# Second attention product as whole float32, two heads side by side on halves of TensorE's columns

## The chip, the cores and the metric

The kernel runs on one core of a Trainium2 chip. The metric is the device time of one execution in microseconds (us). Before the change the median of three runs is 637.88 us (636.99 to 638.83).

## The reference

Attention over pooled keys, then a channel mix (a gated feed-forward with a token shift). B = 8 batches, H = 8 heads, S = 576 tokens, D = 64; keys and values are averaged over groups of 8 tokens, so each head has 72 keys.

```python
k_p = k.reshape(B, H, Sp, pool, D).mean(axis=3)        # Sp = 576 / 8 = 72
v_p = v.reshape(B, H, Sp, pool, D).mean(axis=3)
scores = scale * np.matmul(q, k_p.transpose(0, 1, 3, 2))
attn = softmax(scores)                                  # over the 72 keys
x = np.matmul(attn, v_p)                                # then heads side by side: (B, S, 512)
xk = mu_k * x + (1.0 - mu_k) * x_prev                   # x_prev: x shifted by one token
xr = mu_r * x + (1.0 - mu_r) * x_prev
k = np.maximum(xk @ w_k, 0.0)                           # 512 -> 1024
out = sigmoid(xr @ w_r) * (k * k @ w_v)                 # 1024 -> 512
```

## The kernel before

The 4608 tokens are cut into 12 chunks of 384 (`CHUNKS`, L32). A chunk lies in one batch or, every third, crosses from one to the next (192 tokens each). A chunk has three tiles of 128 tokens; 36 tiles in all. Matrix products of the channel mix are made in a reduced float32 form (`F32R`), with each operand split into a high and a low part and three products for one; chunk 0 alone (`WHOLE`, L35) uses whole float32, since its weights arrive as words that must first be converted.

Per tile: `softmax` (L562) multiplies queries by pooled keys (L582, on TensorE, two heads at a time through a block-diagonal `kbd`), subtracts the maximum, takes exponentials, and multiplies by the reciprocal sums, the first 64 keys of each head into `pm` (L638) and the last eight into `px` (L632). `transposed` (L646) turns `pm` with four TensorE transposes (L657, two heads of 64 keys each fill 128 columns), and copies the result into a high part `pth` (ScalarE, L668) and a low part `ptl` (VectorE, L670). `transposed_rest` (L676) makes three copies of the last eight keys of four heads (`pr`, L688 and L690: high, low, high), turns them with two transposes of 96 columns (L696), and copies them into `ptr` (L703).

Per batch: `values` (L503) sums the pooled values and writes them into block-diagonal `vbd_h` and `vbd_l` (high and low); `last_values` (L536) does so for the last eight keys, in one masked tile `vbd_r` of 96 rows (L549), whose input is loaded three times over (`vr`, L396).

Per chunk and pair of heads g = 0 to 3: `attended` (L707) makes, on TensorE, three products of 128 x 128 (high-high, low-high, high-low) and one of 96 x 128 for the last keys (L739), accumulated in one bank; where a chunk crosses batches, each of the two stretches has its own four. In chunk 0 one whole-float32 product with `vbd_w` takes the place of the three. Then `shifted` (L746) makes the token shift: ScalarE L752, GpSimd L760 to L764, VectorE L771 (`xm`, or `xkh` and `xrh` in chunk 0), and `x_parts` (L783) splits the result. After that come `hidden` (L815: x by w_k), `gate` (L864: x by w_r, sigmoid), and `mixed` (L896: by w_v), whose result is multiplied by the gate (L905) and stored (L909).

Loads are issued on SyncE's queue in the order of the list `LOADS` (L39), then batch by batch; weights are converted by `convert` (L405: ScalarE, then four VectorE operations, L419 to L431) and split by `split` (L440).

The order of the work is set while the program is built. `Order` (L70) runs every step as a thread: a thread names what it needs (`need`), which buffer it takes (`take`), and on which engine the next instructions would run and how long they are reckoned to take. It picks the engine that could start first and, on it, the ready thread with the earliest due time (`tile_due`, `att_due`, `begin`, moved by `EARLIER`). The result is one fixed list of instructions for each engine; on the chip each engine goes through its own list in order and waits on semaphores.

Of the kernel before, what the change touches and what calls it, by code (L numbers as in the profile page):

```python
# [16 lines left out]
P = 128  # L17
# [3 lines left out]
KM = 64  # L21
# [6 lines left out]
REM = 3 * 4 * KR  # L28
# [28 lines left out]
COPIES_ON_ACT = 0  # L57

EARLIER = {
# [3 lines left out]
}  # L63
# [127 lines left out]
def attention_then_channel_mix(  # L191
# [10 lines left out]
    mask: bass.AP,  # L202
# [12 lines left out]
    def slots(kind, n, shape, dtype=F32, pool=None):  # L215
# [6 lines left out]
    mask_sb = const.tile([REM, 4], F32, name="mask_sb")  # L222
# [8 lines left out]
    vbd_h = [const.tile([P, NPAIR, P], F32R, name=f"vbd_h{i}") for i in range(2)]  # L231
    vbd_l = [const.tile([P, NPAIR, P], F32R, name=f"vbd_l{i}") for i in range(2)]
    vbd_w = sb.tile([P, NPAIR, P], F32, name="vbd_w", tag="xkl")
    vbd_r = [const.tile([REM, 2, 4, D], F32R, name=f"vbd_r{i}") for i in range(2)]

# [4 lines left out]
        "pth": [P, NPAIR, CH], "ptl": [P, NPAIR, CH], "ptr": [REM, 2, CH],  # L240
# [3 lines left out]
    def operand(kind, c):  # L244
        if (kind, c) not in operands:
            dtype = F32 if c in WHOLE and kind != "ptr" else F32R
            operands[kind, c] = sb.tile(shapes[kind], dtype, name=f"{kind}_{c}", tag=kind)
        return operands[kind, c]
# [4 lines left out]
    slots("rk", 2, [P, CH])  # L253
    slots("e", 2, [P, 2, 4, KEYS])
    slots("pm", 2, [P, 2, 4, KM])
    slots("px", 2, [P, 2, 4, KR])
    slots("pr", 2, [P, 2, 3, 4, KR], F32R)
    slots("mx", 2, [P, 2, 4, 1])
    slots("sm", 2, [P, 2, 4, 1])
    slots("vq", 1, [REM, 2, D], F32R)  # L260
    slots("tmp", 2, [P, WP])
# [4 lines left out]
    for tag, n in (("sl", 2), ("ptl", 1), ("xrl", 1)):  # L266
# [46 lines left out]
    def constants():  # L313
# [7 lines left out]
        yield "dve", 0.5, False  # L321
        nc.vector.memset(vbd_w, 0.0)
        order.make(("values clear", 0))
        for t in (vbd_h[1], vbd_l[1]):
            yield "pool", 0.5, False
            nc.gpsimd.memset(t.bitcast(F32), 0.0)
        order.make(("values clear", 1))

    def warm():

        zeros = yield take("tmp")
# [7 lines left out]
        order.give("tmp", zeros)  # L339
# [27 lines left out]
    def load(kind, i):  # L367
        if kind == "c":
            yield "sp", 1.0, False
            nc.sync.dma_start(out=mask_sb, in_=mask)  # L370
            nc.sync.dma_start(out=mu_sb, in_=mu)
            order.fetched("mask", 2)
# [32 lines left out]
    def convert(kind, i):  # L405
# [8 lines left out]
        ff = yield take("tmp")  # L414
# [20 lines left out]
        order.give("tmp", ff)  # L435
# [67 lines left out]
    def values(b, p):  # L503
        i = b % 2
        whole = b == 0 and 0 in WHOLE
        yield need(("v", 2 * b + p), ("attended", last_chunk[b - 2]) if b > 1 else ("values clear", b))
# [3 lines left out]
        gs = slice(2 * p, 2 * p + 2)  # L510
        yield "act", 0.41, False
        for h2 in range(2):
            r = slice(h2 * D, (h2 + 1) * D)
            nc.scalar.copy(out=(vbd_w if whole else vbd_h[i])[r, gs, r], in_=o[r])
        if not whole:
            yield "dve", 0.4, True
            for h2 in range(2):
                r = slice(h2 * D, (h2 + 1) * D)
# [5 lines left out]
        if whole:  # L524
            yield need(*[("attended", c) for c in WHOLE])
            yield act(2 * P)
            nc.scalar.copy(out=vbd_h[i][:, gs], in_=vbd_w[:, gs])
            yield dve(2 * P)
            nc.vector.tensor_tensor(
# [116 lines left out]
    def transposed(i):  # L646
# [3 lines left out]
        if c == 1:  # L650
            yield need(("early", "ptl", 0))
# [342 lines left out]
```

## Time and profile before

| | |
|---|---|
| median of 3 runs | 637.88 us (636.99 to 638.83) |
| profiled execution | 637.27 us, of which 635.5 us from the first to the last instruction (its span) |
| granted TensorE clock, mean | 0.997 |
| TensorE busy | 621.6 us (98%) |
| VectorE, ScalarE, GpSimd busy | 413.7, 334.2, 215.2 us (65%, 53%, 34%) |
| DMA engines | about full in the first 50 us, mostly idle after that |

The profile names engines PE (TensorE products), PEld (its weight loads), DVE (VectorE), ACT (ScalarE), POOL (GpSimd) and SP (SyncE; SPq is its queue of issues). Products overlap in TensorE's pipeline, so that the busy time of a group is more than its share of the span: what one costs is read from the distance between the starts of two neighbours. A line such as `128*64 128x144` gives the stationary operand's rows and columns, then the moving one's shape. `[1.11 <-DVE xkh L771]` at a row's end is idle time before it and what ended it.

### The profile page before, as it was taken

The numbers are of one execution on the slowest core, as the hardware profiler recorded it, in microseconds if no ns is written. First come the engines' busy times: TensorE is split into PE (matmuls) and PEld (weight loads), VectorE is DVE, ScalarE is ACT, GpSimd is POOL, SyncE is SP. The second block draws the span as 40 slices with busy tenths as digits, with TensorE's granted clock in tenths as the row PEclk, the third lists the DMA queues.
The fourth block names the chain that finished last, engine by engine and source line by source line (L and its number), as shares of the span: only waits on it lengthen the run. The fifth ranks groups of instructions, "written<-read, shape, count | busy, mean of one in ns | idle before, by whom it ended". The sixth has DMA issues, their size and how long they took to land.

```text
span 635.5 us, 9032 instructions
## 1 busy us (share of the span) xinstructions
PE 621.6 (98%) x3240; PEld 537.8 (85%) x3240; DVE 413.7 (65%) x829; ACT 334.2 (53%) x688; POOL 215.2 (34%) x331
## 2 busy tenths in 40 slices
PE   7899999999999999999999999999999999999997
PEld 6754468889989989989988988988988988988986
DVE  5999998856979537647845665855954654653421
ACT  4667656855665544635554555546555445444420
POOL 1240347464445128018115018316405104203200
PEclk9999999999999999999999999999999999999999
DMA  9991130043314211033011061033110100000001
GB/s 300 369 393 47 32 126 34 17 126 141 92 51 172 60 35 51 0 142 107 17 35 51 0 200 51 17 103 131 33 35 34 34 18 34 18 0 35 17 1 50
DMA packets 34988, 50.91 MB, mean 80 GB/s; under 512 B 6528, under 2 KB 22912, under 8 KB 34944
## 3 DMA queue, kind: packets, MB, share of 16 engines
q1 hardware_dynamic: 34944, 50.35, 23.6%
q8 instruction: 25, 0.41, 0.3%
q14 instruction: 19, 0.16, 0.1%
HBM read 40.90 MB, written 9.44 MB: 79 GB/s over the span
## 4 chain that ended last, share of the span: by engine, by line
PE 81%; DVE 8%; DMA 6%; POOL 2%; issue 1%; ACT 1%; SPq 1%; ACTq 0%; POOLq 0%; DVEq 0%
PE mm L896 28%; PE mm L815 26%; PE mm L864 15%; PE bank L739 5%; PE sc L582 4%; PE bank L657 2%; DMA qs<-in_qT 2%; DMA early_xrl<-in_vm 1%; DMA got_wk<-in_w_k 1%; DMA got_wv<-in_w_v 1%; PE bank L696 1%; DVE tmp L426 1%; DVE tmp L419 1%; DVE pr L688 1%; POOL xrl L789 1%
## 5 line engine op out<-in xcount | busy, mean ns | idle before, releaser
L815 PE MATMUL mm<-xkh,w_k 128*128 128x384 f32 x704 | 182.3, 339 | 0.3 <-ACT xkh L787 0.3
L896 PE MATMUL mm<-w_v,sh 128*128 128x512 f32 x528 | 170.8, 392 | 0.0
L815 PEld LDWEIGHTS mm<-xkh,w_k 128*128 128x128 f32 x704 | 125.6, 188 | 1.9 <-issue 0.6
L815 PE MATMUL mm<-xkl,w_k 128*128 128x384 f32 x352 | 118.2, 336 | 0.7 <-POOL xkl L789 0.7
L896 PEld LDWEIGHTS mm<-w_v,sh 128*128 128x128 f32 x528 | 99.2, 188 | 19.8 <-issue 0.2
L896 PE MATMUL mm<-w_v,sl 128*128 128x512 f32 x264 | 103.0, 390 | 0.0
L632 POOL TENSOR_TENSOR px<-e,sm 128x64 f32<-128x64 f32 x32 | 10.8, 339 | 225.0 <-DVE sm L626 224.8
L864 PE MATMUL mm<-w_r,xrh 128*128 128x512 f32 x264 | 84.9, 394 | 0.0
L752 ACT ACTIVATE t<-bank,om_sb 128x384 f32<-128x384 f32 x96 | 48.8, 582 | 55.9 <-PE bank L739 55.8
L838 ACT CAST sh<-rk 128x384 fp32r<-128x384 f32 x88 | 45.2, 514 | 58.7 <-DVE rk L832 58.7
L771 DVE SCALAR_TENSOR_TENSOR xm<-bank,mu_sb,t 128x384 f32<-128x384 f32 x88 | 51.4, 612 | 35.1 <-POOL t L764 18.3
L840 DVE TENSOR_TENSOR sl<-rk,sh 128x384 fp32r<-128x384 f32 x88 | 53.3, 609 | 25.5 <-ACT sh L838 25.4
L815 PEld LDWEIGHTS mm<-xkl,w_k 128*128 128x128 f32 x352 | 66.1, 188 | 1.3 <-POOL xkl L789 1.3
L905 DVE TENSOR_TENSOR rs<-mm,rs 128x512 f32<-128x512 f32 x36 | 24.8, 689 | 60.7 <-PE mm L896 60.7
L832 DVE SCALAR_TENSOR_TENSOR rk<-mm,rk 128x384 f32<-128x384 f32 x88 | 48.5, 552 | 16.3 <-ACT rk L825 15.9
L864 PEld LDWEIGHTS mm<-w_r,xrh 128*128 128x128 f32 x264 | 49.6, 188 | 10.0
L789 POOL TENSOR_TENSOR xkl<-xm,xkh 128x384 fp32r<-128x384 f32 x44 | 44.8, 1021 | 38.2 <-ACT xkh L787 37.9
L896 PEld LDWEIGHTS mm<-w_v,sl 128*128 128x128 f32 x264 | 49.7, 188 | 9.0
L463 POOL TENSOR_TENSOR stage<-stage 128x512 f32<-128x512 f32 (+5 forms) x60 | 50.7, 852 | 13.7 <-ACT rk L825 5.9
L825 ACT ACTIVATE rk<-mm 128x384 f32<-128x384 f32 x88 | 42.8, 487 | 23.4 <-PE mm L815 22.7
L864 PE MATMUL mm<-w_r,xrl 128*128 128x512 f32 x132 | 51.4, 389 | 0.0
L595 DVE TENSOR_REDUCE mx<-sc 128x8 f32<-128x576 f32 x35 | 26.3, 751 | 32.6 <-PE sc L582 32.6
(115 smaller groups left out, 977.7 us busy)
## 6 DMA issues: line engine op xcount, KB each, us to landing
out<-rs SPq DMA_DIRECT2D x36, 256.0 KB, 2.0
stage<-in_kT SPq DMA_DIRECT2D x15, 576.0 KB, 5.2
qs<-in_qT SPq DMA_DIRECT2D x32, 256.0 KB, 3.2
stage<-in_vm SPq DMA_DIRECT2D x14, 512.0 KB, 6.3
got_wk<-in_w_k SPq DMA_DIRECT2D x8, 512.0 KB, 8.6
got_wv<-in_w_v SPq DMA_DIRECT2D x8, 512.0 KB, 10.0
stage<-in_vr SPq DMA_DIRECT2D x7, 384.0 KB, 4.5
got_wr<-in_w_r SPq DMA_DIRECT2D x4, 512.0 KB, 8.4
```

What stands on the lines that cost most here:

```text
L463: nc_eng.tensor_tensor(out=st[:, :, :w], in0=st[:, :, :w], in1=st[:, :, w:2 * w], op=ALU.add)
L739: nc.tensor.matmul(out=xp[:, o], lhsT=v, rhs=p, start=(q == 0), stop=(q == len(terms) - 1))
L752: nc.scalar.activation(out=t[:, m, 1:n + 1], in_=xp, func=AF.Copy, scale=om_sb[:, m, g:g + 1])
L771: nc.vector.scalar_tensor_tensor(out=xm[:, :n], in0=xp, scalar=mu_sb[:, m, g:g + 1], in1=t[:, m, :n], op0=ALU.mult, op1=ALU.add,)
L789: nc.gpsimd.tensor_tensor(out=lo, in0=xm[:, :n], in1=hi, op=ALU.subtract)
L815: nc.tensor.matmul(out=hp, lhsT=w[:, o], rhs=x[:, ct, :n], start=(ct == 0 and k == 0), stop=(ct == NCT - 1 and k == len(terms) - 1),)
L825: nc.scalar.activation(out=rk[:, :n], in_=hp, func=AF.Relu)
L832: nc.vector.scalar_tensor_tensor(out=rk[:, :n], in0=hp, scalar=0.0, in1=rk[:, :n], op0=ALU.max, op1=ALU.mult)
L838: nc.scalar.copy(out=sh[:, :n], in_=rk[:, :n])
L840: nc.vector.tensor_tensor(out=operand("sl", c)[:, jt, :n], in0=rk[:, :n], in1=sh[:, :n], op=ALU.subtract)
L864: nc.tensor.matmul(out=bank, lhsT=x[:, ct, o], rhs=w, start=(ct == 0 and k == 0), stop=(ct == NCT - 1 and k == len(terms) - 1),)
L896: nc.tensor.matmul(out=bank, lhsT=s[:, o], rhs=w, start=(jt == 0 and k == 0), stop=(jt == NJT - 1 and k == len(terms) - 1),)
```

## The change

The product of probabilities and values is made in whole float32 in every chunk. Values of a batch lie in `val`, 72 keys in the partitions and 64 columns for each head; the probabilities of a tile are multiplied in place in `e` (72 keys of eight heads), turned by eight transposes of 72 columns (two groups of four, each with its bank and one ScalarE copy into `pt`), and used as they are. A product has the 72 keys of one head as its stationary operand's rows and 64 columns; the two heads of a pair write to the lower and the upper 64 partitions of the same bank, one after the other in program order, in pieces of at most 128 tokens. The splits into high and low, the block-diagonal tiles, the separate tile for the last eight keys, its mask and the three-fold load go. The last eight keys of the values are summed in partitions 0 to 31 and copied into partitions 64 to 71 of `val` by four small DMAs on SyncE's queue (`moved`). Working buffers of `convert` and `hidden` become one kind (`rk`), `e` has three buffers in place of two, and `EARLIER` loses its entries for the step that is gone.

```diff
-REM = 3 * 4 * KR
+REM = 4 * KR
+PIECE = 128
-    "transposed_rest 6": 3.3, "hidden 2 5": -0.6, "convert r 1": -1.2, "mixed 0 1": -1.6,
+EARLIER = {'hidden 2 5': -0.6, 'convert r 1': -1.2, 'mixed 0 1': -1.6, 'hidden 2 6': 3.9, 'hidden 2 3': -1.7, 'convert v 6': -1.0, 'keys 1 0': 1.8, 'hidden 1 5': -1.3}
...
+    val = [const.tile([KEYS, NPAIR, 2, D], F32, name=f"val{i}") for i in range(2)]
...
     def values(b, p):
...
-            nc.scalar.copy(out=(vbd_w if whole else vbd_h[i])[r, gs, r], in_=o[r])
-        if not whole:
-            yield "dve", 0.4, True
-            for h2 in range(2):
-                r = slice(h2 * D, (h2 + 1) * D)
-                nc.vector.tensor_tensor(
-                    out=vbd_l[i][r, gs, r], in0=o[r], in1=vbd_h[i][r, gs, r], op=ALU.subtract
-                )
+            nc.scalar.copy(
+                out=val[b % 2][:KM, 2 * p:2 * p + 2, h2], in_=o[h2 * KM:(h2 + 1) * KM]
+            )
...
     def last_values(b):
...
-        for k in range(2):
-            nc.vector.tensor_tensor(
-                out=vbd_r[i][:, k],
...
+        order.add(-25, moved(b, vq))
+
+    def moved(b, vq):
+
+        yield "sp", 2.4, False
+        for q in range(4):
+            nc.sync.dma_start(
+                out=val[b % 2].rearrange("k (r j) h d -> k r (j h) d", r=2)[KM:, :, q],
+                in_=vq[q * KR:(q + 1) * KR],
+            )
+        order.now += 2.5
         order.give("vq", vq)
         order.make(("rest", b))
...
-        yield dve(8 * KR) if v else ("pool", 0.24, True)
-        eng.tensor_tensor(
-            out=px, in0=e[:, :, :, KM:], in1=sm.broadcast_to([P, 2, 4, KR]), op=ALU.mult
+        yield dve(8 * KEYS) if v else ("pool", 1.12, True)
+        (nc.vector if v else nc.gpsimd).tensor_tensor(
+            out=e, in0=e, in1=sm.broadcast_to([P, 2, 4, KEYS]), op=ALU.mult
         )
...
     def transposed(i):
...
-        yield "pe", 0.44, False
-        for g in range(NPAIR):
-            nc.tensor.transpose(
-                out=tp[:, g, :],
-                in_=pm[:, g // 2, (g % 2) * 2:(g % 2) * 2 + 2, :].rearrange("p h k -> p (h k)"),
-                identity=ident,
-            )
...
+        for a in range(2):
+            bank = yield take("bank")
+            tp = bank[:KEYS].rearrange("p (a b) -> p a b", b=P)
+            yield "pe", 0.28, False
+            for h in range(4):
+                nc.tensor.transpose(out=tp[:, h], in_=e[:, a, h], identity=ident)
+            if a:
+                order.give("e", e)
+            yield act(4 * P)
+            nc.scalar.copy(
+                out=operand("pt", c).rearrange("k g h n -> k (g h) n")[:, 4 * a:4 * a + 4, off:off + P], in_=tp
+            )
+            order.give("bank", bank)
         order.make(("main", i))
-
-    def transposed_rest(i):
...
     def attended(c, g):
...
-                terms = [(vh, ph), (vl, ph), (vh, pl)]
-            terms.append((vbd_r[i][:, r, 2 * j:2 * j + 2, :], operand("ptr", c)[:, r, o]))
...
+        pieces = [
+            (b, at + o, min(PIECE, k - o)) for b, _, k, at in units[c] for o in range(0, k, PIECE)
+        ]
...
+        for b, o, k in pieces:
+            for h in range(2):
                 nc.tensor.matmul(
-                    out=xp[:, o], lhsT=v, rhs=p, start=(q == 0), stop=(q == len(terms) - 1)
+                    out=xp[h * D:(h + 1) * D, o:o + k], lhsT=val[b % 2][:, g, h],
+                    rhs=operand("pt", c)[:, g, h, o:o + k], start=True, stop=True,
                 )
```

How this moves the lists of the engines is seen in three places. The first is the start of TensorE's list, from the last transposes of chunk 0 to its first hidden product (L815 before, L711 after; L657, L696 and L602 are transposes, L739 and L634 attended products, L582 and L539 scores). Before:

```order
L657 MATMUL bank_115<-ident,pm_90 128x128 x4
L696 MATMUL bank_113<-ident,pr_94 96x128 x2
L739 MATMUL bank_114<-pth_232,vbd_w 128x384
L739 MATMUL bank_114<-ptr_241,vbd_r_76 128x384
L739 MATMUL bank_115<-pth_232,vbd_w 128x384
L739 MATMUL bank_115<-ptr_241,vbd_r_76 128x384
L582 MATMUL sc_112<-kbd_69,qs_103 128x144 x4
L815 MATMUL mm_118<-xkh_354,got_wk_136 128x384
```

After:

```order
L602 MATMUL bank_102<-ident,e_84 72x128 x4
L602 MATMUL bank_100<-ident,e_84 72x128 x4
L539 MATMUL sc_99<-kbd_68,qs_90 128x144 x4
L634 MATMUL bank_101<-pt_207,val_70 64x128 x6
L634 MATMUL bank_102<-pt_207,val_70 64x128 x6
L711 MATMUL mm_105<-xkh_352,got_wk_122 128x384
```

The scores of the next tile now stand ahead of the first attended products, which are followed directly by hidden products. The second place is in the middle of TensorE's list, where the first attended products of chunk 2 stand between the products by w_v (L896, then L792) of chunk 1. Before:

```order
L896 MATMUL mm_116<-w_v_1076,sh_842 128x512
L739 MATMUL bank_114<-pth_873,vbd_h_72 128x384
L739 MATMUL bank_114<-pth_873,vbd_l_74 128x384
L739 MATMUL bank_114<-ptl_874,vbd_h_72 128x384
L739 MATMUL bank_114<-ptr_883,vbd_r_77 128x384
L739 MATMUL bank_113<-pth_873,vbd_h_72 128x384
L739 MATMUL bank_113<-pth_873,vbd_l_74 128x384
L739 MATMUL bank_113<-ptl_874,vbd_h_72 128x384
L739 MATMUL bank_113<-ptr_883,vbd_r_77 128x384
L896 MATMUL mm_117<-w_v_931,sh_842 128x512
```

After:

```order
L792 MATMUL mm_104<-w_v_822,sl_855 128x512
L792 MATMUL mm_104<-w_v_822,sh_832 128x512
L634 MATMUL bank_100<-pt_883,val_71 64x128 x6
L634 MATMUL bank_102<-pt_883,val_71 64x128 x6
L792 MATMUL mm_104<-w_v_857,sh_832 128x512
```

Eight full-width products become twelve half-width ones (each of two instructions, since they are whole float32), and they stand in the middle of a tile's products by w_v. The pairs g = 0 and 1 are neighbours in every chunk and g = 2 and 3 stand alone (in one chunk with a neighbour), which makes 35 such stretches in the program. The third place is SyncE's list, some 24 issues from the start, between the loads of w_k, w_r (got_wr) and queries (qs). Before:

```order
L387 DMA got_wk_270<-in_w_k 128x1024
L379 DMA qs_104<-in_qT 128x4x64 x2
L387 DMA got_wr_291<-in_w_r 128x1024
L379 DMA qs_105<-in_qT 128x4x128
L387 DMA got_wr_304<-in_w_r 128x1024
```

After:

```order
L365 DMA got_wk_253<-in_w_k 128x1024
L357 DMA qs_91<-in_qT 128x4x64 x2
L365 DMA got_wr_269<-in_w_r 128x1024
L357 DMA qs_92<-in_qT 128x4x128
L507 DMA val_70<-vq_89 8x2x64 x4
L365 DMA got_wr_302<-in_w_r 128x1024
```

The four DMAs that complete batch 0's values stand behind the same loads of keys, queries, values and weights that stood there before (of which the two of the last eight keys are a third as large).

More of the change, by code (lines that the diff above doesn't have):

```diff
@@ L265, in attention_then_channel_mix @@
     early = {}
-    for tag, n in (("sl", 2), ("ptl", 1), ("xrl", 1)):
+    for tag, n in (("sl", 2), ("xkl", 1), ("xrl", 1)):
         t = sb.tile([P, n, 2 * POOL * KEYS], F32, name=f"early_{tag}", tag=tag)
@@ L320, in constants @@
             order.make(("kbd clear", b))
[L321 to L327, printed above, removed]
     def warm():
-        zeros = yield take("tmp")
+        zeros = yield take("rk")
         yield "dve", 0.5, False
@@ L338, in warm @@
         order.give("bank", bank)
-        order.give("tmp", zeros)
+        order.give("rk", zeros)
     def complements():
@@ L434, in convert @@
         )
-        order.give("tmp", ff)
+        order.give("rk", ff)
         order.make(("full", kind, i))
@@ L503, in values @@
     def values(b, p):
-        i = b % 2
-        whole = b == 0 and 0 in WHOLE
-        yield need(("v", 2 * b + p), ("attended", last_chunk[b - 2]) if b > 1 else ("values clear", b))
+        yield need(("v", 2 * b + p), *([("attended", last_chunk[b - 2])] if b > 1 else []))
         if not b:
@@ L522, in values @@
         done_with(kind, raw)
         order.make(("values", b, p))
[L524 to L528, printed above, removed]
-            nc.vector.tensor_tensor(
-                out=vbd_l[i][:, gs], in0=vbd_w[:, gs], in1=vbd_h[i][:, gs], op=ALU.subtract
-            )
-            order.make(("value parts", b, p))
-        else:
-            order.make(("value parts", b, p))
@@ L641, in softmax @@
-        order.give("e", e)
+        yield dve(8 * KEYS) if v else ("pool", 1.12, True)
+        (nc.vector if v else nc.gpsimd).tensor_tensor(
+            out=e, in0=e, in1=sm.broadcast_to([P, 2, 4, KEYS]), op=ALU.mult
+        )
         order.give("sm", sm)
-        held["pm", i] = pm
-        order.make(("pm", i))
+        held["e", i] = e
+        order.make(("e", i))
     def transposed(i):
         c, off, _ = tiles[i]
-        o = slice(off, off + P)
-        yield need(("pm", i), *([("attended", c - 1)] if c else []))
@@ L650, in transposed @@
-        if c == 1:
-            yield need(("early", "ptl", 0))
-        pm = held.pop(("pm", i))
-        bank = yield take("bank")
-        tp = bank.rearrange("p (a b) -> p a b", b=P)
-        yield "pe", 0.44, False
-        for g in range(NPAIR):
-            nc.tensor.transpose(
-                out=tp[:, g, :],
-                in_=pm[:, g // 2, (g % 2) * 2:(g % 2) * 2 + 2, :].rearrange("p h k -> p (h k)"),
-                identity=ident,
-            )
-        order.give("pm", pm)
-        yield act(NPAIR * P)
@@ L710, in attended @@
         whole = c in WHOLE
-        mine = [i for i, t in enumerate(tiles) if t[0] == c]
-        yield need(*[(k, i) for i in mine for k in ("main", "side")])
+        yield need(*[("main", i) for i, t in enumerate(tiles) if t[0] == c])
         yield need(
-            "om", *[("rest", b) for b, *_ in units[c]],
-            *[("values" if whole else "value parts", b, p) for b, *_ in units[c] for p in range(2)],
+            "om", *[("rest", b) for b, *_ in units[c]], *[("values", b, p) for b, *_ in units[c] for p in range(2)]
         )
```

110 lines of the change are left out of this document (12 added, 98 removed), and 2 rows, old and new, of the table EARLIER.

## Prediction

> **What bounds the kernel now.** I read the page first: its head gives the span and the busy time of each engine.
>
> ```profile
> span 635.5 us, 9032 instructions
> PE 621.6 (98%) x3240; PEld 537.8 (85%) x3240; DVE 413.7 (65%) x829; ACT 334.2 (53%) x688; POOL 215.2 (34%) x331
> ```
>
> TensorE (PE) is busy for 98% of the span. A busy PE need not be at its peak, so I looked next at stretches (columns: PE, weight loads, VectorE, ScalarE, GpSimd, then the granted clock, the DMA share and GB/s).
>
> ```profile
> 15.00:20.00 5.00, 4.94 (x32) 4.71 (x31) 4.49 (x17) 2.20 (x10) 0.00 (x0) 0.72 1.02 388
> 25.00:50.00 25.00, 22.64 (x75) 13.73 (x76) 24.39 (x51) 16.91 (x39) 11.44 (x18) 1.00 1.03 368
> 125.00:635.00 510.00, 506.67 (x2730) 457.09 (x2728) 301.85 (x590) 255.32 (x507) 169.22 (x262) 1.00 0.18 59
> ```
>
> From 125 us on PE idles 3.3 us out of 510, while VectorE has 208 us to spare: there the time is PE's own work, and whatever the other engines save is worth nothing. Only in the first 50 us do others count: VectorE is busy 24.4 of 25 us, and the DMA engines are full (share 1.03). So the change is priced as PE steps in the long part, and as waits in the first part. A step is the distance between the starts of two neighbours on PE, because printed durations overlap.
>
> **The attended product.** These rows of the timeline (start, duration) hold one head pair of a chunk with 384 tokens of one batch (four products, the next line's start ends the last), one chunk that crosses a batch (16 products of 192, first and end), and one pair of chunk 0.
>
> ```profile
> 138.62 0.34 PE L739 MATMUL bank<-pth,vbd_h 128*128 128x384 f32 x1
> ...
> 139.32 0.39 PE L896 MATMUL mm<-w_v,sh 128*128 128x512 f32 x1
> ```
>
> ```profile
> 232.08 0.25 PE L739 MATMUL bank<-pth,vbd_h 128*128 128x192 f32 x1
> ...
> 233.84 0.41 PE L896 MATMUL mm<-w_v,sh 128*128 128x512 f32 x1
> ```
>
> ```profile
> 26.17 0.81 PE L739 MATMUL bank<-pth,vbd_w 128*128 128x384 f32 x2
> ...
> 26.99 1.15 PE L582 MATMUL sc<-kbd,qs 128*128 128x144 f32 x8
> ```
>
> That is 0.70 us a pair, 1.76 us for two pairs (0.88 each), and 0.82 us. Seven chunks of the first kind, four of the second and chunk 0, four pairs each: 28 x 0.70 + 16 x 0.88 + 4 x 0.82 = 37.0 us are removed.
>
> What replaces them uses 64 of the 128 columns for each head. The kernel does this already at four score tiles that cross a batch, so the trace has both forms of the same work: eight full-width instructions of 144, and sixteen half-width ones.
>
> ```profile
> 145.47 1.14 PE L582 MATMUL sc<-kbd,qs 128*128 128x144 f32 x8
> 146.35 0.60 PE L815 MATMUL mm<-xkh,w_k 128*128 128x384 f32 x2
> 146.79 0.34 PE L815 MATMUL mm<-xkl,w_k 128*128 128x384 f32 x1
> ```
>
> ```profile
> 181.50 0.39 PE L896 MATMUL mm<-w_v,sh 128*128 128x512 f32 x1
> 181.82 1.20 PE L582 MATMUL sc<-kbd,qs 128*64 128x144 f32 x16
> 182.96 0.50 PE L896 MATMUL mm<-w_v,sh 128*128 128x512 f32 x1
> 183.29 0.39 PE L896 MATMUL mm<-w_v,sl 128*128 128x512 f32 x1
> ```
>
> Full width: 146.79 - 145.47 = 1.32, less two ordinary steps of 0.174 (a quarter of the 0.70 above) leaves 0.97, or 0.122 for each instruction. Half width: 183.29 - 181.50 = 1.79, less the two ordinary steps of 0.23 around it, is 1.33. So sixteen half-width instructions cost as much as eight full ones, i.e. two run at a time, plus 0.35 us for going into the half-width form and coming out. This 0.35 is the first number that speaks against the change. A whole-float32 product is two instructions; a piece of 128 tokens for both heads is then two paired steps of 0.122 x 128/144 = 0.108, or 0.217 us. There are 128 such pieces and 32 of 64 tokens. The latter lie between 0.108 (half the stream) and 0.217 (no shorter than a 128); I take 0.115, since 64 weight columns and 64 tokens are both half. Streams: 128 x 0.217 + 32 x 0.115 = 31.5 us. The program order has 35 separate stretches of these products (two head pairs together, the others alone): 35 x 0.35 = 12.3 us. Sum: 31.5 + 12.3 - 37.0 = **+6.8 us**, from -5.5 (the visits cost nothing) to +10.1 (64 tokens cost as 128).
>
> The Trainium skill, "TensorEngine Tiling (Array Packing)", section Theoretical Speedup, gives up to 2x for an output side of 64 or less. By that alone this term would be -5.5 and the sum below 646.6; the same page's Key Properties say that changing the mode drains TensorE, and the 0.35 of the row is what I go by.
>
> **The transposes.** Before, a tile needs four of 128 columns and two of 96; now eight of 72.
>
> ```profile
> 155.84 0.60 PE L657 MATMUL bank<-ident,pm 128*128 128x128 f32 x4
> 156.19 0.59 PE L815 MATMUL mm<-xkh,w_k 128*128 128x384 f32 x2
> 156.62 0.34 PE L815 MATMUL mm<-xkl,w_k 128*128 128x384 f32 x1
> 156.80 0.38 PE L696 MATMUL bank<-ident,pr 128*96 128x128 f32 x2
> 156.93 0.60 PE L815 MATMUL mm<-xkh,w_k 128*128 128x384 f32 x2
> 157.37 0.34 PE L815 MATMUL mm<-xkl,w_k 128*128 128x384 f32 x1
> ```
>
> ```profile
> L657 PE MATMUL bank<-ident,pm 128*128 128x128 f32 x144 | 21.7, 275 | 0.2 <-DVE pr L688 0.2
> L696 PE MATMUL bank<-ident,pr 128*96 128x128 f32 x72 | 13.8, 273 | 0.5 <-DVE pr L690 0.4
> ```
>
> 156.62 - 155.84 - 0.35 = 0.43 for four, and 157.37 - 156.80 - 0.35 = 0.22 for two: 0.108 and 0.11 each. The one with 96 stationary columns is no cheaper than the one with 128; both stream the 128 columns of the identity, and so will the new ones. So I take 0.109: 36 tiles x 8 x 0.109 = 31.4, against 36 x 0.65 = 23.4: **+8.0 us**. If instead the price went with the stationary columns, 72/128 x 0.109 = 0.061, it would be 17.6, or -5.8 us. I take the first, because 96 columns lie nearest to 72 and show no gain.
>
> The Trainium skill, "TensorE: Matmul & The Clock Gate", sections LDWEIGHTS and Back-to-back issue gap, says that a weight load takes its columns / 1.2 ns and that the spacing in a stream is set by load and product together. An estimate from it is 60 ns for 72 columns, which would make this term -6.1 and the sum below 644.8; that it would give 80 ns for the 96 columns where the row has 110 speaks against it here.
>
> **The last eight keys of the values.** Before, they have products of their own; now they are copied into partitions 64 to 71 by four small DMAs on SyncE's queue, and every attended product waits for them. For batch 0 these stand behind 26 loads. Rows of SyncE's issues, what became of the load just ahead (last number: us to landing), and a DMA of 1.5 KB in the same crowd:
>
> ```profile
> 29.85 0.54 SPq L379 DMA_DIRECT2D qs<-in_qT  x1
> 30.43 2.45 SPq L387 DMA_DIRECT2D got_wr<-in_w_r  x3
> ```
>
> ```profile
> qs<-in_qT SPq DMA_DIRECT2D x1, 256.0 KB, 6.9
> ```
>
> ```profile
> mask_sb<-in_mask SPq DMA_DIRECT2D x1, 1.5 KB, 8.5
> ```
>
> The load ahead of the four is issued at 29.85 and lands at 36.75. The change drops 2 x 256 KB ahead of it (the value tail was loaded three times over), which at the 388 GB/s above is 1.3 us: 35.4. By the small DMA's 8.5 us from 29.1 it would be 37.6. I take 35.4, from the row directly ahead. Now PE's start:
>
> ```profile
> 25.24 0.91 PE L739 MATMUL bank<-pth,vbd_w 128*128 128x384 f32 x2 [0.49 <-ACT pth L665]
> 29.25 1.56 PE L815 MATMUL mm<-xkh,got_wk 128*128 128x384 f32 x4 [1.11 <-DVE xkh L771]
> 37.98 15.10 PE L815 MATMUL mm<-xkh,got_wk 128*128 128x384 f32 x46 [1.02 <-DVE xkh L771]
> 56.93 3.27 PE L864 MATMUL mm<-got_wr,xrh 128*128 128x512 f32 x7 [1.27 <-DVE got_wr L431]
> ```
>
> Attended begins at 25.24 before, and at 35.4 now: 10.2 us in which PE, whose next work is the hidden product of its output, has nothing else. Queued behind the wait are the token shift on ScalarE and VectorE, and behind these the conversions of the later weights. VectorE comes out with less to do, so the waits of 1.11, 1.02 and 1.27 go: 10.2 - 3.4 = **+6.8 us**, from -3.4 (the rows land in time) to about +12: 37.6 instead of 35.4, with the waits half kept. The granted clock of 0.72 at 15 to 20 us, after a PE gap, lost 1.4 us; this may come again and is in the upper end.
>
> **Hidden or free.** VectorE loses groups like these two (50.6 us); GpSimd has one multiplication for two.
>
> ```profile
> L688 DVE CAST pr<-px 128x64 fp32r<-128x64 f32 x72 | 28.1, 433 | 5.8 <-POOL px L632 5.8
> L670 DVE TENSOR_TENSOR ptl<-bank,pth 128x512 fp32r<-128x512 f32 x33 | 22.5, 685 | 7.3 <-ACT pth L668 7.2
> ```
>
> After 125 us PE waits for none of them: nought. ScalarE copies 512 columns twice a tile where it copied 512 and 256, and is busy half its time. The later batches' four DMAs wait on SyncE for the summed tail; query loads and output stores stand behind them. Their values are due a chunk later (a twelfth of the span, 53 us), which hides them; without that cover seven batches would pay some 4 us each: four issues like the 0.54 above and then a landing like that of an output store in an idle queue.
>
> ```profile
> out<-rs SPq DMA_DIRECT2D x36, 256.0 KB, 2.0
> ```
>
> **Sum.** The profiled execution took 637.27 us, 1.77 more than its span and 0.6 under the median of 637.88. 637.3 + 6.8 + 8.0 + 6.8 = **658.9 us**.
>
> **Rivals.** (1) Transposes priced by stationary columns, the rest as above: 637.3 + 6.8 - 5.8 + 6.8 = 645.1. For it: the smaller load (the rule of the Trainium skill on weight loads, above, points there); against it the two rows at 0.108 and 0.11. (2) The tail's rows land in time or early work elsewhere covers them: 652.1, or 650 with half of the 3.4 us won. Against it: 26 loads ahead and full DMA engines. (3) Faster: the transposes are priced by their columns at 0.061, in the 288 places on PE, and the tail is not late: 637.3 + 6.8 - 5.8 - 3.4 = 634.9. It decides from 0.063 us a transpose downward; at 0.069 it is a draw. (4) The change doesn't do what it says: the two heads run one after the other, 31.5 us of streams twice: 690. The sixteen half-width instructions in 1.33 us speak against it.
>
> **Chances.** Forecast 0.55 (own range 653 to 667), rival 1 0.15, rival 2 0.13, rival 3 0.07, rival 4 0.03, mixtures 0.07 (among them visits that cost nothing, 646.6, with 0.03). The range 644 to 668 leaves out 3, 4, some mixtures and a tail of the forecast, 0.2. A measurement of this kernel can tell about 0.3% (1.9 us) from no change. Faster by more: 0.08 (rival 3 and a little); within: 0.04; slower: 0.88.
>
> **What would show it.** Right: half-width stretches of L634 that lie 0.35 us further apart than their streams; L602 at 0.109 us a step; PE idle before the first L634 until a DMA into val lands at some 35 us. Wrong: L602 steps near 0.06; PE entering L634 before 28 us; L634 steps not in pairs; new idle time on PE after 125 us.

## The result, and the profile after

The change makes the kernel slower: 672.72 us median of 4 runs (670.34 to 674.79) against 637.53 (636.99 to 638.83) of the kernel before beside it, a ratio of 1.0558 [1.0538, 1.0578]. The forecast was 658.9; its range ended at 668. The profiled execution took 671.94 us, its span is 670.2.

First the head of the page after the change:

```profile
span 670.2 us, 9733 instructions
PE 643.4 (96%) x3700; PEld 540.5 (81%) x3700; DVE 353.2 (53%) x629; ACT 341.1 (51%) x684; POOL 212.2 (32%) x297
```

VectorE has 60.5 us less to do. TensorE is 21.8 us longer busy, but the span grew by 34.7: about 13 us are new idle time. The windows say where (PE first, the granted clock third from the end):

```profile
26.20:43.20 17.00, 10.54 (x50) 7.22 (x50) 9.88 (x18) 5.93 (x13) 5.01 (x14) 0.51 0.98 333
...
25.00:50.00 25.00, 17.42 (x80) 11.46 (x81) 16.27 (x30) 10.71 (x24) 7.93 (x17) 0.66 0.99 347
...
165.00:170.00 5.00, 3.09 (x15) 2.45 (x14) 2.86 (x5) 2.51 (x6) 3.73 (x6) 0.93 0.23 59
170.00:175.00 5.00, 5.00 (x23) 5.00 (x22) 3.94 (x9) 2.50 (x6) 4.41 (x6) 0.73 0.62 168
125.00:670.00 545.00, 537.16 (x3183) 469.27 (x3181) 257.41 (x454) 268.50 (x519) 171.10 (x239) 1.00 0.16 51
```

From 25 to 50 us the clock is at 0.66 where it was at 1.00, and for 17 us of it at half. After 125 us PE idles 545.00 - 537.16 = 7.8 us, where it idled 3.3. The stretch at 165 us is new: PE busy 3.09 of 5 us, and a lower clock in the next 5.

What PE waits for, longest first (us in total, times, longest):

```profile
PE bank L634 <- DMA val<-vq: 5.7, 1, 5.7
PE mm L711 <- ACT xkh L683: 5.0, 4, 1.5
...
PE mm L711 <- POOL xkl L685: 2.5, 6, 0.5
```

The first row was forecast. The other two, 7.5 us in ten waits of the hidden product for the parts of x, were not.

**Where the 34.7 us lie.** The hidden product of a chunk is a good landmark, since each chunk has it once. Its first instruction in the first and fourth chunk, before (the first is the row at 29.25 in the prediction) and after, from the timelines:

```profile
199.57 0.43 PE L815 MATMUL mm<-xkh,w_k 128*128 128x384 f32 x1
```

```profile
34.06 2.91 PE L634 MATMUL bank<-pt,val 72*64 72x128 f32 x24 [5.66 <-DMA val<-vq]
37.78 1.65 PE L711 MATMUL mm<-xkh,got_wk 128*128 128x384 f32 x2 [0.80 <-DVE xkh L667]
...
217.91 0.44 PE L711 MATMUL mm<-xkh,w_k 128*128 128x384 f32 x1
```

That cuts the span in three: A up to the first landmark, B from there to the fourth chunk's, C to the end. The right columns put the prediction's terms into these stretches: visits at 0.35 (12 in B with what precedes it, 23 in C), transposes at 0.109 (100 for 80, 188 for 136), the streams' -5.5 shared out by instructions (-1.8, -3.7), and in A and B the terms of the start (10.2 - 1.11, then -2.3). Visits and transposes are counted in the two traces. So are the score products: the new list puts 16 of them (two tiles) behind the fourth landmark that stood ahead of it (80 in B and 144 in C before, 64 and 160 after); at the prediction's 0.122 each they move 1.95 us from B to C.

| stretch | before | after | longer by | by the prediction's terms | left over |
|---|---|---|---|---|---|
| A | 29.25 | 37.78 | 8.5 | 9.1 | -0.6 |
| B | 170.32 | 180.13 | 9.8 | 4.2 + 2.2 - 1.8 - 2.3 - 1.95 = 0.35 | 9.5 |
| C | 435.93 | 452.29 | 16.4 | 8.05 + 5.7 - 3.7 + 1.95 = 12.0 | 4.4 |

So the start came as forecast, and some 14 us were missing from the sum, 9.5 in B and 4.4 in C, long after the start.

### The profile page after: what moved, and what is told of

It reads as the page before. It is cut to its first block, busy times and chain, and to the rows that moved or that the text cites. A ratio compares the mean times of both kernels' runs of the same rounds, so it can differ in the third digit from the quotient of the medians.

```text
span 670.2 us, 9733 instructions
## 1 busy us (share of the span) xinstructions
PE 643.4 (96%) x3700; PEld 540.5 (81%) x3700; DVE 353.2 (53%) x629; ACT 341.1 (51%) x684; POOL 212.2 (32%) x297
## 4 chain that ended last, share of the span: by engine, by line
PE 80%; DVE 9%; POOL 4%; issue 3%; ACT 2%; DMA 1%; ACTq 0%; POOLq 0%; DVEq 0%
PE mm L792 27%; PE mm L711 27%; PE mm L760 13%; PE bank L602 4%; PE bank L634 4%; PE sc L539 4%; DVE rk L404 2%; DVE xm L667 2%; POOL xrl L685 1%; POOL xkl L685 1%; DVE rk L397 1%; POOL stage L441 1%; DMA val<-vq 1%; ACT t L648 1%; DVE mx L552 1%
## 5 line engine op out<-in xcount | busy, mean ns | idle before, releaser
L711 PE MATMUL mm<-xkh,w_k 128*128 128x384 f32 x704 | 185.6, 345 | 5.0 <-ACT xkh L683 5.0
L792 PE MATMUL mm<-w_v,sh 128*128 128x512 f32 x528 | 177.9, 401 | 0.0
L711 PEld LDWEIGHTS mm<-xkh,w_k 128*128 128x128 f32 x704 | 126.6, 191 | 6.9 <-ACT xkh L683 6.3
L711 PE MATMUL mm<-xkl,w_k 128*128 128x384 f32 x352 | 120.2, 342 | 2.6 <-POOL xkl L685 2.5
L792 PEld LDWEIGHTS mm<-w_v,sh 128*128 128x128 f32 x528 | 99.1, 188 | 23.8 <-issue 3.8
L586 POOL TENSOR_TENSOR e<-e,sm 128x576 f32<-128x576 f32 x32 | 37.2, 1162 | 209.2 <-DVE sm L583 196.3
L792 PE MATMUL mm<-w_v,sl 128*128 128x512 f32 x264 | 103.0, 390 | 0.0
L736 DVE TENSOR_TENSOR sl<-rk,sh 128x384 fp32r<-128x384 f32 x88 | 57.1, 653 | 37.5 <-ACT sh L734 37.5
L667 DVE SCALAR_TENSOR_TENSOR xm<-bank,mu_sb,t 128x384 f32<-128x384 f32 x88 | 51.5, 612 | 39.7 <-POOL t L660 25.9
L711 PEld LDWEIGHTS mm<-xkl,w_k 128*128 128x128 f32 x352 | 67.0, 190 | 5.3 <-POOL xkl L685 5.3
L606 ACT COPY pt<-bank 72x512 f32<-72x512 f32 x72 | 40.9, 577 | 35.7 <-PE bank L602 35.6
L760 PEld LDWEIGHTS mm<-w_r,xrh 128*128 128x128 f32 x264 | 49.6, 188 | 10.1
L792 PEld LDWEIGHTS mm<-w_v,sl 128*128 128x128 f32 x264 | 49.7, 188 | 8.7
L441 POOL TENSOR_TENSOR stage<-stage 128x512 f32<-128x512 f32 (+5 forms) x60 | 53.8, 904 | 3.3 <-DMA stage<-in_vm 1.6
```

What stands on the lines that cost most here:

```text
L441: nc_eng.tensor_tensor(out=st[:, :, :w], in0=st[:, :, :w], in1=st[:, :, w:2 * w], op=ALU.add)
L606: nc.scalar.copy(out=operand("pt", c).rearrange("k g h n -> k (g h) n")[:, 4 * a:4 * a + 4, off:off + P], in_=tp)
L667: nc.vector.scalar_tensor_tensor(out=xm[:, :n], in0=xp, scalar=mu_sb[:, m, g:g + 1], in1=t[:, m, :n], op0=ALU.mult, op1=ALU.add,)
L711: nc.tensor.matmul(out=hp, lhsT=w[:, o], rhs=x[:, ct, :n], start=(ct == 0 and k == 0), stop=(ct == NCT - 1 and k == len(terms) - 1),)
L736: nc.vector.tensor_tensor(out=operand("sl", c)[:, jt, :n], in0=rk[:, :n], in1=sh[:, :n], op=ALU.subtract)
L760: nc.tensor.matmul(out=bank, lhsT=x[:, ct, o], rhs=w, start=(ct == 0 and k == 0), stop=(ct == NCT - 1 and k == len(terms) - 1),)
```

## The experiments

Each ran beside the kernel before in three rounds; that had a median between 637.16 and 637.23 us each time. "Gain" is against the changed kernel's 672.72.

**Theory.** The missing 14 us are waits of the hidden product for the x parts of the chunk's last head pair, because the new list puts that pair too close ahead. **Rivals:** GpSimd or VectorE hold the x parts up; the clock lost at the start carries on; the visits or the transposes cost more than reckoned.

What the theory is read from: the timeline rows of the last attended pair of the third chunk and of that chunk's hidden product, before (140.00, with the landmark at 146.35 quoted in the prediction) and after.

```profile
140.00 0.34 PE L739 MATMUL bank<-pth,vbd_h 128*128 128x384 f32 x1
```

```profile
160.59 0.39 PE L792 MATMUL mm<-w_v,sh 128*128 128x512 f32 x1
160.91 0.88 PE L634 MATMUL bank<-pt,val 72*64 72x128 f32 x12
161.71 0.50 PE L792 MATMUL mm<-w_v,sh 128*128 128x512 f32 x1
162.05 0.39 PE L792 MATMUL mm<-w_v,sl 128*128 128x512 f32 x1
...
163.40 0.61 PE L711 MATMUL mm<-xkh,w_k 128*128 128x384 f32 x2
...
167.19 0.62 PE L711 MATMUL mm<-xkh,w_k 128*128 128x384 f32 x2 [1.45 <-ACT xkh L683]
168.27 0.44 PE L711 MATMUL mm<-xkl,w_k 128*128 128x384 f32 x1 [0.46 <-POOL xkl L685]
```

Before, 6.35 us of PE's list lie between the two; now 2.5. The chain of waits in the same place shows what has to fit into that time (start, us, what):

```profile
163.33 1.11 POOL e L586
164.44 1.37 POOL stage L441
...
165.98 0.63 DVE xm L667
...
166.63 0.52 ACT xkh L683
...
167.22 1.01 POOL xkl L685
```

The shift of the last pair stands on GpSimd behind a normalisation (1.11) and a pooling sum (1.37); from there to the low part it takes 2.4 us more.

**attended_earlier** tries the distance and leaves every engine's amount of work as it is.

```diff
+EARLIER.update({f'attended {c} {g}': -3 for c in range(1, 12) for g in range(4)})
```

> The due times of the attended products of chunks 1 to 11 are put 3 us earlier, so that the last pair of a chunk stands some 11 us of TensorE's work ahead of the chunk's first hidden product, where it stands 2.3 to 2.5 us ahead in chunks 2, 4, 8 and 10 of the changed kernel (and 6 to 7 in the kernel before). Nothing is computed otherwise. Theory: the waits of the hidden product for the last x parts after 100 us (7 to 9 us with the slow clock behind them) come from this short distance; they go, and the time is 663 to 667. Rival (the x parts are late because GpSimd and VectorE are held by the new longer operations, wherever the product stands): the waits stay, and the time is within 2 us of 672.7.

Measured: 661.73 us (661.16 to 662.48), ratio 1.0378 [1.0357, 1.04]; a gain of 11.0, a little more than expected. Timeline rows (the first landmark; last pair and hidden product of the third chunk; the fourth chunk's landmark) and the longest of what is left of the waits for x's parts behind the first chunk's:

```profile
38.90 1.65 PE L712 MATMUL mm<-xkh,got_wk 128*128 128x384 f32 x2 [0.80 <-DVE xkh L668]
...
158.63 0.88 PE L635 MATMUL bank<-pt,val 72*64 72x128 f32 x12
164.30 0.43 PE L712 MATMUL mm<-xkh,w_k 128*128 128x384 f32 x1
...
216.24 0.42 PE L712 MATMUL mm<-xkh,w_k 128*128 128x384 f32 x1
```

```profile
PE mm L712 <- POOL xkl L686: 1.1, 3, 0.5
```

The pair is 5.7 us ahead here (about 11, as expected, in the eight chunks after it), and the waits that are left lie in the second chunk, at 106 to 113 us. Stretch C is 660.7 - 216.24 = 444.46, or 8.5 more than before; with this list's 21 visits and 180 transposes there (and 144 score products, as before) the terms give 7.35 + 4.8 - 3.7 = 8.45. Nothing is left over in C. The clock at its start is as low (0.51 from 25 to 46 us), and C closes all the same; and C closes with the prediction's prices for visits and transposes.

GpSimd and VectorE had as much work as in the changed kernel, so their load is not the cause. But their order moved with the list. ScalarE makes the high part of the same last pair, before and in this run, at:

```profile
144.47 0.51 ACT L787 CAST xkh<-xm 128x384 fp32r<-128x384 f32 x1 [0.57 <-DVE xm L771]
...
162.28 0.52 ACT L684 CAST xkh<-xm 128x384 fp32r<-128x384 f32 x1 [0.69 <-DVE xm L668]
```

From the pair's start to the end of this part it took 5.0 us before, 6.2 after the change (160.91 to 167.15) and 4.2 here. So in this chunk the new list shortened the distance by 3.9 us and lengthened the chain by 1.2; the run takes back most of the one and all of the other, and doesn't separate them. Over the ten chunks from the third on, the changed kernel has this part ready 1.1 to 3.1 us ahead of the hidden product's start in five, up to 1.0 behind it in two, and 2.2 to 3.8 behind it in three; only in these three does the profile show a wait for it, of 0.5 to 1.9 us. In this run the part is 1.5 to 7.7 us ahead in all ten.

**list_by_measured_prices** asks whether the list is short because the planner reckons 0.1 us for entering and leaving the half-width form and 0.28 us for four transposes.

```diff
-            yield "pe", 0.28, False
+            yield "pe", 0.44, False
...
-        yield "pe", 0.1 + sum(2 * max(0.111, k / 1200 + 0.003) for _, _, k in pieces), False
+        yield "pe", 0.36 + sum(k / 590 for _, _, k in pieces), False
```

> The changed kernel with nothing but the planner's two prices put right: 0.44 instead of 0.28 us for four transposes, 0.36 + tokens / 590 instead of 0.1 + tokens / 600 for a pair. The list then has 29 stretches of half-width products instead of 35 and only two chunks (instead of five) whose last pair stands under 4 us of PE work ahead of the hidden product. Theory (the waits after 125 us come from the list, and the list is wrong since the planner takes a visit for 0.1 us): 6 x 0.36 = 2.2 less by visits and 4 to 6 less by waits, 665 (663 to 667). Rival (the list is not short because of the prices, or the waits come from elsewhere): 670 to 673.

Measured: 667.07 us (666.03 to 667.5), ratio 1.046 [1.0434, 1.0486]: at the edge of what was expected. The waits of L711 for xkh and xkl are 2.9 us in three and 2.5 in four, 5.4 in all against 7.5 in ten. Its first hidden product comes 2.5 us later (40.25); from there on it is 6.9 us shorter than the changed kernel, of which six visits fewer make 2.1.

The prices are a part of the cause. Even with them the planner does not put all of these pairs early; that it lacks the delay of the engines behind them is a guess that no run tested.

**full_width_product** and **fewer_transposes_earlier** and **full_width_and_earlier** measure the terms. The first and third make the product with both heads' 128 value columns at once, the second leaves transposes out.

```diff
-            for h in range(2):
-                nc.tensor.matmul(
-                    out=xp[h * D:(h + 1) * D, o:o + k], lhsT=val[b % 2][:, g, h],
-                    rhs=operand("pt", c)[:, g, h, o:o + k], start=True, stop=True,
-                )
+            nc.tensor.matmul(
+                out=xp[:, o:o + k], lhsT=val[b % 2][:, g].rearrange("k h d -> k (h d)"),
+                rhs=operand("pt", c)[:, g, 0, o:o + k], start=True, stop=True,
+            )
```

```diff
-            for h in range(4):
+            for h in range(1 if a else 4):
...
-                out=operand("pt", c).rearrange("k g h n -> k (g h) n")[:, 4 * a:4 * a + 4, off:off + P], in_=tp
+                out=operand("pt", c).rearrange("k g h n -> k (g h) n")[:, 4 * a:4 * a + 4, off:off + P],
+                in_=tp[:, 0:1].broadcast_to([KEYS, 4, P]) if a else tp,
```

> One product of all 128 columns stands for each pair of half-width ones; it leaves out the second head's own probabilities (both heads get the first's), so the streams are as long as those of two half-width products side by side, and only the 35 visits to the half-width form go. Theory: each visit costs 0.35 to 0.39 us, so 12.6 us go and the time is 660 (658 to 662). Rival (half-width products are dear in their streams, or the visits cost only where PE waits anyway): a gain under 8 us.

Measured: 666.89 us (666.25 to 667.56), ratio 1.0462 [1.0443, 1.0481]; a gain of 5.8 where 11 to 15 were expected. Its waits for x grew from 7.5 to 9.2 us:

```profile
PE mm L710 <- ACT xkh L682: 6.0, 4, 2.1
...
PE mm L710 <- POOL xkl L684: 3.2, 9, 0.5
```

So part of what a cheaper step saves ahead of a late operand is waited away again, here some 1.5 us of 7.3, as the next run shows. Most of the rest of the miss is the pieces of 64 tokens, which cost more at full width (below) and which this expectation had left out. The term had to be measured in a list without these waits:

> The attended products earlier by 3 units, and the product of both heads as one full-width instruction over 128 value columns (left out: the second head's own probabilities; the first head's are used for both). Without waits that take it back, the entry into and exit from the half-width form should now be seen whole: 33 stretches x 0.36 us = 11.9 less, against 32 x 2 pieces of 64 tokens that cost 0.109 an instruction alone instead of about 0.055 a step in pairs, 3.3 more: 661.7 - 8.6 = 653 (652 to 655). Rival (the 0.35 is overlap with neighbours that the trace draws apart, no time of its own): 660 to 665.

Measured: 654.43 us (653.56 to 655.55), ratio 1.0274 [1.0248, 1.0299]: 7.3 less than attended_earlier, as expected within its range. One pair at full width, and the landmark:

```profile
153.87 0.39 PE L792 MATMUL mm<-w_v,sh 128*128 128x512 f32 x1
154.10 0.83 PE L634 MATMUL bank<-pt,val 72*128 72x128 f32 x6
154.69 0.48 PE L792 MATMUL mm<-w_v,sh 128*128 128x512 f32 x1
155.00 0.39 PE L792 MATMUL mm<-w_v,sl 128*128 128x512 f32 x1
...
211.77 0.42 PE L711 MATMUL mm<-xkh,w_k 128*128 128x384 f32 x1
```

From the row before the pair to the second behind it: 155.00 - 153.87 = 1.13 us, and 162.05 - 160.59 = 1.46 in the half-width rows above. A visit costs 0.33 us more than the same streams at full width. In C the two kernels differ by 444.46 - (651.8 - 211.77) = 4.4 us; 21 visits of 0.33 are 6.9, and most of the rest is what pieces of 64 tokens take back: read stretch by stretch, the 15 without such pieces are 0.31 to 0.34 longer at half width, the six with them 0.10 shorter, 4.3 in all.

> The attended products earlier by 3 units, and three of the four transposes of each tile's second group left out (left out: these heads' own probabilities; the first head's transpose is copied to all four). 36 x 3 = 108 transposes fewer. Theory (0.109 us each, by the 128 columns that stream): 11.8 less than 661.7, 650 (649 to 651.5). Rival (0.061 us each, by the 72 stationary columns, the rest of the step being overlap): 6.6 less, 655.

Measured: 654.28 us (651.63 to 655.15), ratio 1.0259 [1.0228, 1.0289]: 7.4 less, which would be the rival's 6.6. But the trace says that the start took part of it back (first pair, and the landmark):

```profile
34.54 2.94 PE L636 MATMUL bank<-pt,val 72*64 72x128 f32 x24 [7.35 <-DMA val<-vq]
...
216.75 0.42 PE L713 MATMUL mm<-xkh,w_k 128*128 128x384 f32 x1
```

With fewer transposes PE is at the wait earlier and stands there 7.35 us instead of 4.8. In C, which has no such wait, the difference is 444.46 - (653.2 - 216.75) = 8.0 us for 72 transposes: 0.111 each. The total alone would have shown the wrong price.

**The start.** The next kernels move batch 0's four small DMAs off SyncE's queue.

```diff
-            nc.sync.dma_start(
+            (nc.sync if b else nc.scalar).dma_start(
```

> The four small copies of batch 0's last eight keys are issued on ScalarE's queue in place of SyncE's, where they no longer stand behind 26 loads; the list of every engine is otherwise that of the changed kernel (672.7 us, profiled execution 671.9). Theory: the first attended product starts at 34.06 us only because of that place in SyncE's list; now it starts at 27 to 29 us, the long stretch at half clock (26 to 43 us) goes too, and the time falls by 6 to 10 us, to 663 to 667. Rival (the rows come late through the full DMA engines whatever queue issues them): the start stays above 32 us and the time within 2 us of 672.7.

Measured: 668.14 us (665.79 to 671.63), ratio 1.0486 [1.0447, 1.0526]; a gain of 4.6, less than expected. In its trace (of the fastest run, 665.79) PE enters the product at 28.18, as expected, and then waits for VectorE:

```profile
28.18 2.83 PE L634 MATMUL bank<-pt,val 72*64 72x128 f32 x24
33.67 1.65 PE L711 MATMUL mm<-xkh,got_wk 128*128 128x384 f32 x2 [2.66 <-DVE xkh L667]
...
22.47 3.51 ACTq L507 DMA_DIRECT2D val<-vq  x4
26.02 1.23 ACT L395 ACTIVATE rk<-got_wk 128x512 f32<-128x512 f32 x2 [3.04 <-DMA val<-vq]
```

ScalarE issues the four for 3.5 us; the conversion of two weights that stands behind them in its list is late, and VectorE has eight steps of these conversions ahead of the first x part.

> Batch 0's four tail DMAs on ScalarE's queue and the attended products of chunks 1 to 11 placed 3 units earlier in the list, together. Alone the two gained 4.6 and 11 us. Theory (two separate causes: the start, and the distance between a chunk's last attended pair and its hidden product): the gains add, 657 us (656 to 659), and after 125 us no wait of the hidden product over 0.5 us is left. Rival (the early gain is handed on to whatever waits next, as conversions late behind ScalarE's queue): 660 to 662.

Measured: 658.62 us (658.24 to 659.62), ratio 1.0336 [1.0315, 1.0358]: 3.1 less than attended_earlier, within what was expected if the two causes are separate.

> As the run before, but batch 0's four DMAs are issued by GpSimd. Theory (the loss in the run with ScalarE's queue came from ScalarE standing still for the issues and the token shift behind it, not from the place of the loads): PE enters the attended product at 27 to 30 us, the wait for the x parts after it is under 1.5 us instead of 2.7, and the time is 654 to 656. Rival (VectorE's chain of the first chunk is the limit whoever issues): the same as with ScalarE's queue, within 1 us.

Here the four are issued with `nc.gpsimd` in the same place. Measured: 658.62 us (657.18 to 659.12), ratio 1.033 [1.0307, 1.0353]: no better, as the rival has it (VectorE's chain is the limit whoever issues). But PE enters the product only at 30.00, and VectorE is held in another way:

```profile
25.66 4.02 DVE L398 TENSOR_SCALAR rk<-rk 128x512 f32<-128x512 f32 x2 [0.60 <-ACT rk L396]
...
24.48 2.40 POOL L508 DMA_DIRECT2D val<-vq  x4 [22.64 <-ACT vq L500]
26.90 1.27 POOL L442 TENSOR_TENSOR early_xrl<-early_xrl 128x512 f32<-128x512 f32 x1
28.12 1.27 POOL L442 TENSOR_TENSOR stage<-stage 128x512 f32<-128x512 f32 x1
```

The second of the two conversion steps takes 3.44 of these 4.02 us, from 26.24 on, where the first takes 0.43, and it ends 0.3 us after GpSimd's second sum does; the run with ScalarE's queue has 0.98 for such a pair. The Trainium skill, "SBUF — State Buffer", section SBUF: two separate sides, says that VectorE in its two-port modes and GpSimd lock one pair of ports for a whole instruction, and the other one blocks. The 3.44 us beside GpSimd's sums fit that, but no run separates it from another cause.

Then the x parts were put ahead of two of the conversions, with the planner told who issues the four (here ScalarE; the other kernel has `"pool", 2.4`, 1.5 and `nc.gpsimd`):

```diff
+EARLIER.update({f'attended {c} {g}': -3 for c in range(1, 12) for g in range(4)})
+EARLIER.update({'convert k 2': 6, 'convert k 3': 6})
...
-        yield "sp", 2.4, False
+        yield ("sp", 2.4, False) if b else ("act", 3.4, False)
...
-        order.now += 2.5
+        order.now += 2.5 if b else 0.5
```

> Batch 0's four tail DMAs on ScalarE's queue, attended products 3 units earlier (as in the run of both, 658.6), and besides the planner is told that the tail comes by ScalarE and that two of the weights are converted 6 units later: VectorE's list has fewer conversion steps ahead of the first x part. Theory (what is left at the start, first hidden product at 35.0 us instead of 29.25, is the conversions in VectorE's list ahead of the x parts): first hidden product at 31 to 32.5 us, time 654 to 656. Rival (the wait only moves on to the hidden products of the two late weights): first hidden product early, then waits for got_wk on PE, time 658 to 660.

> As the run before, with the four DMAs on GpSimd and the planner told so. Same theory: 654 to 656. GpSimd's issue of four DMAs took 2.4 us and VectorE's two first conversion steps stood 4.0 us beside it and the pooling sums behind it; if that holds VectorE again, the time stays 657 to 659 (rival).

Measured: 656.29 us (653.79 to 657.37), ratio 1.0291 [1.0261, 1.032], and 655.84 us (654.99 to 657.32), ratio 1.0292 [1.0267, 1.0317]: some 2.5 less than without, at and a little above the upper end of 654 to 656. The first hidden product came at 33.06 (ScalarE), a little later than expected, and only at 35.28 with GpSimd, so that the second kernel did not do it in the way expected; its gain lies in B. Its timeline:

```profile
35.28 2.62 PE L713 MATMUL mm<-xkh,got_wk 128*128 128x384 f32 x4
...
209.86 0.42 PE L713 MATMUL mm<-xkh,w_k 128*128 128x384 f32 x1
```

**busy_through_wait** puts 18 products of the identity into the wait at the start, to keep the clock up.

```diff
+        if c == 0 and g == 0:
+            for _ in range(18):
+                nc.tensor.matmul(out=bank[:, :P], lhsT=ident, rhs=ident, start=True, stop=True)
```

> Eighteen products of the identity with itself, written to a bank that the first attended product then overwrites, fill TensorE's wait for the last eight keys of batch 0. Theory: the granted clock is back at full before the attended products start, where it was half until 43 us; the work between 34 and 43 us gets faster and the time falls by 2 to 4 us, to 669 to 671. Rival (that work waits for VectorE and ScalarE, not for TensorE's clock): the same time within 1 us, or later by what the added products take.

Measured: 671.94 us (669.6 to 673.29), ratio 1.0538 [1.0509, 1.0566]; no gain, so the rival holds. The clock by windows:

```profile
30.00:35.00 5.00, 4.39 (x46) 4.20 (x45) 1.54 (x3) 0.00 (x0) 0.00 (x0) 0.98 0.95 290
35.00:40.00 5.00, 3.58 (x28) 2.22 (x24) 3.43 (x6) 3.59 (x8) 3.56 (x9) 0.70 1.01 385
```

It is full while the added work runs and falls right after it, with the next gap; and ScalarE does nothing from 30 to 35 us, VectorE 1.5 us' worth, all the same, because what they wait for is the product's result.

**all_mended** joins the x parts ahead of the conversions (ScalarE) and the measured prices.

> The run with the x parts ahead of the conversions by ScalarE's queue, and the planner's two prices put right: 27 stretches instead of 32. If a visit costs 0.36 us in a list with no waits left, 1.8 less than that run: 652 to 654. Rival (fewer visits mean that pairs stand together and wait for banks): no less. Either way above the kernel before, since 27 visits (9.7), transposes (7.9) less streams (5.5) leave 12 us with every wait gone: 649 at the least.

Measured: 656.62 us (655.16 to 658.28), ratio 1.0302 [1.0273, 1.0332]: a miss; it can't be told from the run without the prices (1.0291). Its fourth chunk's hidden product begins at 209.62, so C takes 653.4 - 209.62 = 443.8, 0.7 less than in attended_earlier. Four visits and four transposes fewer make 1.8, but eight score products more stand in C (152 for 144), which are 1.0, so that 0.8 was due. From its first hidden product (33.79) to the end the profiled run takes 619.6 us, and the run without the prices 621.6 from 33.06; five visits fewer make 1.75. So behind the start the visits saved are won; 0.7 us of it is lost at the start, and the total, whose runs spread over 3 us, doesn't show the rest. No version of the changed kernel came near the one before: of the 18.6 us that the best one is slower, 13.6 are the terms of the change itself (8.45 in C, 5.1 in B, below).

## Why the prediction failed, step by step

The direction was right, and the bounds of three terms held. The size was wrong by 13.8 us, and the step that failed is this sentence: "After 125 us PE waits for none of them: nought." It took what the kernel before shows, 3.3 us of idle PE after 125 us, for something that spare time on the other engines secures. What hid their chain was mainly the place of the last attended pair in PE's list, 6.35 us ahead of the hidden product, and the change rebuilds that list (and with it the order on GpSimd, which made the chain 1.2 us longer there). Moving these pairs back ahead brought 11.0 us. VectorE's 60 us less earned nothing that shows, as forecast: C closes without them. The other engines' delay, not their load, is what PE waits for.

- **Attended product, +6.8.** Held. The rows at 160.59 to 162.05 give 1.46 - 2 x 0.23 (ordinary steps) - 6 x 0.109 (paired streams) = 0.35 a visit, there are 35, and stretch C closes with this price.
- **Transposes, +8.0.** Held: rival 1, priced by stationary columns, is out. The timeline after the change, read as before:

```profile
183.49 0.60 PE L602 MATMUL bank<-ident,e 128*72 128x128 f32 x4
183.84 0.59 PE L711 MATMUL mm<-xkh,w_k 128*128 128x384 f32 x2
184.27 0.34 PE L711 MATMUL mm<-xkl,w_k 128*128 128x384 f32 x1
```

  184.27 - 183.49 - 0.35 = 0.43 for four, 0.108 each, with 72 stationary columns as with 96 and 128; leaving 72 of them out gave 0.111 each. The Trainium skill, "TensorE: Matmul & The Clock Gate", section LDWEIGHTS, gives the weight load alone columns / 1.2 ns, from which the estimate of 60 ns came. The trace doesn't agree with that as the price of a step: 0.108 us with 72 columns.
- **Last eight keys, +6.8.** The entry was right: 34.06 us for 35.4, after a wait of 5.66 for the DMA. SyncE's row shows the four, issued behind the loads:

```profile
28.83 3.84 SPq L507 DMA_DIRECT2D val<-vq  x4
```

  The way there was right only in part. The sum let the four land with the load ahead of them, 6.9 us after that load's issue, and gave their own issue no time; the row has 3.84 us of issue, and PE starts 1.4 us after its end. That the two nearly cancel is luck. (The upper end's 8.5 us is of a DMA issued at 5.24 us, not among the loads at 29 us.)

  The part "the waits of 1.11, 1.02 and 1.27 go" was half right. They go, but PE meets new ones 50 us later, at 100 to 115 us, and the low clock (0.66 over 25 us, in the bound but not in the sum) adds to them; stretch B is 9.5 us over. Setting the list right brought 2.8 (216.24 - 38.90 = 177.34), with eight transposes more in it, which are 0.9, and 16 score products more, which are 1.95: 5.6 for the same work, so 3.9 stay over. With the 8.5 of A, the 3.9 and the -2.3 this term is 10.1, inside its bound of 12. The x parts ahead of the conversions brought another 2.8: with both, B takes 174.58 us (209.86 - 35.28, GpSimd's run), 4.3 more than before, where visits, transposes and streams give 11 x 0.35 + 28 x 0.109 - 1.8 = 5.1, and 2.8 if the two old waits count as gone. How much of it was the clock and how much the conversions was not separated.
- **Signals.** L602 at 0.109, L634 in pairs, entry at 34 us: right, and with them rival 2 (tail in time), rival 3 (faster) and rival 4 (one head after the other) are out. "New idle time on PE after 125 us" was named as a sign of error, and it is the one that came.

What stays open is the start: with every mending the first hidden product is still 3.8 to 6 us later than before, and no kernel without the four DMAs was run; their issue alone took 2.4 us (GpSimd) to 3.8 us (SyncE). One rival there is untested: `convert` and `hidden` now share two buffers (`rk`), where each had two of its own.

## What to carry to other kernels

A wait that a trace doesn't show is hidden by a distance in some engine's list: when a change rebuilds the list, measure that distance anew (here by building both lists and adding up the steps between an operand's last producer and its first user) before putting "nought". Price a term in a stretch that has no wait which can take it back, and count all of the engine's instructions on both sides of it first (here two tiles' scores had changed sides, 1.95 us); by totals the transposes came out at 0.069 us, by the stretch at 0.111. And a planner needs the new steps' measured prices, though these alone didn't mend it here.

## What the runs showed of the hardware

- Half-width products in whole float32 ran in pairs down to 64 tokens (0.109 us a pair of 128 tokens, 0.058 of 64), but each visit to the form cost 0.35 us (0.33 against the same streams at full width); 35 visits, 12.3 us, cost more than the 5.5 us by which the streams got shorter.
- The granted clock was at half for 17 us around PE's wait at the start, and at 0.73 from 170 to 175 us, behind waits of 1.45 and 0.46 us at 167 and 168 us, though PE was busy in all of these 5 us. The same two waits at 475 and 477 us were not followed by a lower clock (1.00 from 475 to 485 us).
- With the four DMAs on ScalarE's queue (issued from 22.5 to 26.0 us), SyncE issued none of its own loads from 19.7 to 25.9 us. The profile puts 6.2 us of that down to a load of queries (`qs`), so the rows don't show that ScalarE's issue held it.
